# A retention layer and a leaky-ReLU layer on one core: the order of the products around the state sums, the first loads and the last bank

## The chip, the core and the metric

The kernel runs on one core of a Trainium2 chip. Its engines work side by side, each through its own queue in order: TensorE (PE; PEld is its loading of weights), VectorE (DVE), ScalarE (ACT), GpSimd (POOL) and SyncE (SP). SP and ACT also issue the DMAs in these runs. The metric is the device time of one execution in microseconds. Four runs of the kernel before gave 659.25, 658.70, 659.18 and 659.21, with a median of 659.19.

## The reference

Two layers in a row. The first is a recurrent retention over 768 steps, for 4 batch rows with 8 heads of 64 dimensions; the second is a pair of matrix products with a leaky ReLU between them, over the 3072 tokens of the first.

```python
for t in range(S):
    state = gamma[None, :, None, None] * state + np.einsum('bhd,bhe->bhde', k[:, :, t], v[:, :, t])
    y[:, :, t] = scale * np.einsum('bhd,bhde->bhe', q[:, :, t], state)
...
h = x @ w_in
g = np.maximum(0.01 * h, h)
return (g @ w_out).astype(np.float32)
```

## The kernel before

**Chunks and parts.** The sequence is cut into NC = 6 chunks c of 128 steps. For each chunk and each batch row b, the retention is four groups of small f32 products. `score` (L161) multiplies q and k within the chunk, and DVE masks the result (`masked`). `reads` (L215) multiplies q with the state of the chunk before; it uses 64x64 tiles of the array. `last_values` (L252) multiplies the scores with v for the second half of the chunk, with 128 rows and 64 columns of the array. `first_values` (L237) does it for the first half, with 64x64 tiles. `state` (L262) sums k times v for the new state, again with 128 rows and 64 columns; in the last chunk its loop is empty, because nobody needs that state. reads, both kinds of values and the state sums of one row share one tile in PSUM (`sums_at`): the tokens lie in a part of it, the state sums in another. A memset on POOL (`between`) stands between the reads of a row and its first_values, which waits for it. Afterwards DVE scales the tokens into x (`tokens_taken`) and updates the state (`state_taken`).

**The second layer.** 512 tokens of a chunk make a matrix x of 4 blocks. Both products of the second layer use a scheme of seven block products instead of eight, written in `seven` (L555) as M1 to M7; it needs sums and differences of blocks, which DVE makes. `hidden` is the first product with the leaky ReLU, `output` the second. The results of the seven go through four banks of PSUM, A to D. Names in the profile follow: A_h is bank A of hidden, C_o bank C of output. In the very first part of the work plain products are used instead (`direct`, shown as d at L599). In the last output of all, bank C is split in two: its two halves of 256 columns are two tiles, and after M3, the last product, each half is added and stored by itself (`takes_half`). M5 is the other product in that bank.

**Weights.** They arrive as 64-bit words. ACT makes the power of two of each number in three operations (`powers`, L485, at L495, L497 and L498), DVE the mantissa in three (L507, L512 and L519). A piece is 512 KB; the first four pieces are all that direct needs.

**Order.** The order is written by hand. Each engine's queue follows the order in which the code calls. The start is a straight list of calls (L744 to L857): loads, first scores, a product `spread` that spreads a table of decays over the partitions, its copy to `dec` (L821), which tokens_taken reads, then values, powers and mantissas of the first pieces. Chunk 1 is written out too, with `products_in_turn` (L863), which is called for rows 0 and 1 and then for rows 2 and 3. Chunks 2 to 5 use `visit` (L367), called for rows 0 and 1 of chunk 2 and rows 2 and 3 of chunk 5 in the midst of an output, and `visit_with_scores` for the others; the latter makes the state sums in a bank of its own, after last_values.

**Loads at the start.** SP issues q and k of row 0, v of row 0, weight pieces 0 and 1 and so on; ACT issues q and k of row 1, the table of decays and v of row 1 (L761). POOL multiplies v of rows 0 and 1 with their decays (L150) before PE uses it.

Of the kernel before, what the change touches and what calls it, by code (L numbers as in the profile page):

```python
# [9 lines left out]
FP32 = mybir.dt.float32  # L10
# [8 lines left out]
C = 128  # L19
# [4 lines left out]
def kernel(  # L24
# [38 lines left out]
    nc = tc.nc  # L63
    NC = S // C
# [3 lines left out]
    N = B * C // 2  # L68
# [5 lines left out]
    psum = ctx.enter_context(  # L74
        tc.tile_pool(name="psum", bufs=2, space=bass.MemoryType.PSUM))

    mask = const.tile([128, 3, C // 2], FP32, name="mask")
    dec = const.tile([128, HP * C + H + HP], FP32, name="dec")
# [28 lines left out]
    def block(k, i):  # L107

        if k < N_UNITS - 1:
            return unit(k)[:, i]  # L110
        return units[k][i // 2][:, i % 2] if i < 6 else last_s4[:, 0]
# [24 lines left out]
    def load_v(c, b, queue=nc.sync):  # L136
        queue.dma_start(out=heads[c, b][1][:, 1], in_=kv[c, b][:, 1])
# [20 lines left out]
    def two_banks(name):  # L158
        return psum.tile([128, 2, HP, C], FP32, tag="att", bufs=2, name=name)
# [55 lines left out]
    def reads(c, b):  # L215
        x = heads[c, b][0]
        ps = sums_at[c, b] = two_banks(f"yp_{c}_{b}")
        for j, m, i, a in pairs:
            mm = nc.tensor.matmul(ps[ts(i, 64), j, m, :], lhsT=st[b][ts(j, 64), a, :],  # L219
                                  rhs=x[ts(j, 64), 0, a, :], start=(m == 0), stop=False,  # L220
                                  skip_group_check=True)


        reads_done[c, b] = nc.gpsimd.memset(between, 0.0).ins
        tc.add_manual_dep(reads_done[c, b], mm.ins.name, IN_ORDER, reason="rows of the array")
# [3 lines left out]
    between = const.tile([128, 1], FP32, name="between")  # L229

    def values(c, b):
        if c == 0:
            sums_at[c, b] = two_banks(f"yp_{c}_{b}")
        last_values(c, b)
        first_values(c, b)
# [26 lines left out]
    def state(c, b):  # L262
        y = heads[c, b][1]
        sp = for_state(sums_at[c, b])
        for a in range(HP) if c < NC - 1 else ():
            sums_of(sp, y, a)
# [99 lines left out]

    def visit(c, b):  # L367

        for f in (reads, last_values, first_values, state):
            for i in range(2):  # L370
                f(c, b + i)
        for i in range(2):
            tokens_taken(c, b + i, xs[c][0])
        for i in range(2):
            state_taken(c, b + i, for_state(sums_at[c, b + i]))
        for i in range(2):
            if c + 1 < NC:
                ahead(c + 1, b + i)
# [69 lines left out]
            raws[n] = place.bitcast(I64)  # L448
        nc.sync.dma_start(out=raws[n], in_=weights[n])

    def next_powers(scratch=None):
        n = done["powers"]
        done["powers"] += 1
        if n < N_PIECES and f64:
            powers(n, scratch)

    def begin_mantissas(between=None):

# [23 lines left out]

    zs = {}

    def powers(n, scratch):  # L485

        top = raws[n].bitcast(U16).rearrange("p (h n four) -> p h n four", four=4, h=2)[:, :, :, 3]  # L490
        z = zs[n] = work.tile([128, 2, W // 2], I16, tag="z", bufs=3, name=f"z{n}")
        x = piece(n) if scratch is None else scratch


        nc.scalar.activation(x, top, AF.Prelu, alpha=float(BEND), scale=1.0 / 16,  # L495
                             bias=-7.5 / 16 - TOP)
        nc.scalar.activation(z, x, AF.Prelu, alpha=1.0 / BEND, bias=-float(BEND))  # L497
        nc.scalar.activation(z.bitcast(U16), z, AF.Relu, scale=128.0, bias=32768.0)  # L498

# [22 lines left out]
    def plus(out, a, b):  # L522
        nc.vector.tensor_tensor(out=out, in0=a, in1=b, op=ALU.add)  # L523
# [28 lines left out]
    ORDER = (0, 1, 2, 3, 4, 5, 6)  # L552
    FIRST = (0, 4, 1, 2, 3, 5, 6)

    def seven(tiles, name, takes, takes_half=None, order=ORDER):  # L555

        banks = {}  # L560
        which = [("M1", "A", 0, 0), ("M6", "B", 5, 5), ("M5", "C", 4, 4), ("M4", "D", 3, 6),
                 ("M2", "A", 2, 2), ("M7", "B", 1, 1), ("M3", "C", 6, 3)]
        for m, bank, sa, sb in (which[i] for i in order):
            first = bank not in banks
            split = takes_half is not None and bank == "C"
            if first and split:
                banks[bank] = [two_banks(f"{bank}{i}_{name}")[:, 0].rearrange("p a t -> p (a t)")[:, 0:N]
                               for i in range(2)]
            elif first:
                banks[bank] = psum.tile([128, 2, N], FP32, tag="ff", bufs=4, name=f"{bank}_{name}")  # L570
            ps = banks[bank]
            for i in range(2):
                half = ps[i] if split else ps[:, i, :]
                for n, (w, x, t) in enumerate(tiles):
                    rhs = x[:, sb] if sb < 4 else t[:, sb - 4]
                    for k in range(2):
                        nc.tensor.matmul(  # L577
                            half, lhsT=block(w, sa)[:, k, ts(i, 128)], rhs=rhs[:, k, :],
                            start=(first and (i == 0 or split) and n == 0 and k == 0),
                            stop=(n == len(tiles) - 1 and k == 1), skip_group_check=True)  # L580
                if split and m == "M3":
                    takes_half(i, half)
            if not (split and m == "M3"):
                takes(m, ps)
            yield
# [56 lines left out]
    def output(c, o, parts, first, final):  # L642

        got = {}
        at = f"{c}_{parts[0][0]}"

        def store(i):
            if final:
                nc.sync.dma_start(out=out[c, i], in_=o[:, i])

        def takes(m, ps):
            if m == "M1":
                got["m1"] = temp("m1", at)
                nc.scalar.copy(out=got["m1"], in_=ps)
            elif m == "M6":
                got["u2"] = temp("u2", at)
                plus(got["u2"], got["m1"], ps)
                if not first:
                    plus(o[:, 1], got["u2"], o[:, 1])
            elif m == "M5":  # L660
                got["m5"] = temp("m5", at)
                if first:
                    nc.scalar.copy(out=got["m5"], in_=ps)
                elif isinstance(ps, list):
                    for i in range(2):
                        plus(got["m5"][:, i], o[:, 3, i], ps[i])
                else:
                    plus(got["m5"], o[:, 3], ps)
            elif m == "M4":
                if first:  # L670
                    nc.scalar.copy(out=o[:, 2], in_=ps)
                else:
                    plus(o[:, 2], o[:, 2], ps)
            elif m == "M2":
                if first:
                    nc.scalar.copy(out=o[:, 0], in_=ps)
                else:
                    plus(o[:, 0], o[:, 0], ps)
                store(0)
            elif m == "M7":  # L680
                u3 = got["m1"]
                plus(u3, u3, ps)
                plus(o[:, 3], u3, got["m5"])
                store(3)
                plus(o[:, 2], u3, o[:, 2])
                store(2)
            elif m == "M3":
                plus(o[:, 1], got["u2"] if first else o[:, 1], ps)
                store(1)

        def takes_half(i, ps):
            plus(o[:, 1, i], o[:, 1, i], ps)
            nc.sync.dma_start(out=out[c, 1][:, i], in_=o[:, 1, i])

        return seven([(2 * u + 1, g, gd) for u, g, gd in parts], f"o{at}", takes,
                     takes_half if final and c == NC - 1 else None)


    def tile_x(c):
# [50 lines left out]
    x, t = xs[0]  # L750
    rows = t[:, 1:3].rearrange("p i k n -> p (i k n)")[:, 0 : decay.shape[1]]
    nothing = t[:, 0, 0, 0:64].bitcast(BF16)
    half = decay.shape[1] // 2
# [4 lines left out]
    nc.vector.memset(rows[:, half:], 0.0)  # L758
    nc.scalar.dma_start(out=rows[0:H], in_=decay)
    load_v(0, 0)  # L760
    load_v(0, 1, nc.scalar)  # L761
    load_piece(0)
    load_piece(1)
    load_qk(0, 2)
# [11 lines left out]
    for s in range(2):  # L776
        part = mask[ts(s, 64), 0 : 3 - s : 2 - s]
# [22 lines left out]
    spread = psum.tile([128, 2, N], FP32, tag="ff", bufs=4, name="spread")  # L800
# [3 lines left out]
    def scratch(name, n):  # L804
        return work.tile([128, 2, N], FP32, tag=name, name=f"{name}_x{n}")
# [12 lines left out]
    masked(0, 1)  # L818
    nc.tensor.matmul(spread.rearrange("p i n -> p (i n)"), lhsT=place, rhs=g_q, start=True,
                     stop=True, skip_group_check=True)  # L820
    nc.scalar.copy(out=dec[:, 0:n_gq], in_=spread.rearrange("p i n -> p (i n)"))  # L821
    values(0, 0)
    values(0, 1)
    next_powers(scratch("m1", 0))
    begin_mantissas(lambda: taken(0, 0, x))
    taken(0, 1, x)
    end_mantissas()
# [33 lines left out]
        masked(1, b)  # L861

    def products_in_turn(b):  # L863
        reads(1, b)
        values(1, b)
        reads(1, b + 1)
        values(1, b + 1)
        state(1, b)
        state(1, b + 1)

# [24 lines left out]
    next(later)  # L897
    last_sum(0)
    next_mantissas()
    products_in_turn(2)  # L900
    next_powers()
    run(steps, {})
    tokens_taken(1, 2, x1)
# [143 lines left out]
```

## Time and profile before

| What | Value |
|---|---|
| median of four runs | 659.19 us |
| the profiled execution's own time | 659.25 us |
| its span, first to last instruction | 657.4 us |
| granted TensorE clock | 1.000 |
| scores and tables, first products done | 5.70 to 9.5 us |
| PE's waits, all together | 2.2 us |
| last product ends | about 654.2 us |
| last store issued, span ends | 654.71, 657.4 us |

The span is what the profile shows of the execution; 1.85 us of the execution's own time lie outside it. PE's waits of 2.2 us fall into five places, all in the first 20 us. A row of the profile names the line of the code, the engine, the operation, and the tiles written and read; in a row of matmuls, "x16" counts passes, and a product in f32 takes two passes.

### The profile page before, as it was taken

To read this page: it belongs to the slowest core of one execution; us is meant where nothing else is said; L and a number is where in the kernel's file an instruction comes from. 1 tells how busy PE (TensorE), PEld (TensorE's weight loads), DVE (VectorE), ACT (ScalarE), POOL (GpSimd) and SP (SyncE) were. 2 spreads that over 40 slices of the span, in tenths; PEclk is the share of its full clock that TensorE was granted. 3 is DMA by queue.
4 is the path that set the end of the run, shared out by engine and by line. 5 is a ranking of instruction groups with operands and counts; after the bars stand their busy time and mean duration, and the time that the engine had idled before them with its cause. 6 is when DMAs were issued, how large, how long until landed. Compare 5 with 4: busy or idle time off the path is not lost.

```text
span 657.4 us, 11325 instructions
## 1 busy us (share of the span) xinstructions
PE 651.9 (99%) x4921; PEld 568.6 (86%) x4921; DVE 359.9 (55%) x587; ACT 176.3 (27%) x323; POOL 23.1 (4%) x45
## 2 busy tenths in 40 slices
PE   8999999999999999999999999999999999999998
PEld 5888888888888888888888889888888888888886
DVE  4779969889888674243436414526423344431342
ACT  4854555264261002202102211300220210211210
POOL 2000000000001020001001001001000100000000
PEclk9999999999999999999999999999999999999999
DMA  9921322322322650030022003005001001000001
GB/s 340 405 94 33 128 65 77 116 65 94 130 66 81 239 195 0 1 120 10 1 93 101 1 1 129 1 17 178 0 1 58 8 1 49 17 0 1 1 0 64
DMA packets 15761, 48.98 MB, mean 75 GB/s; under 512 B 1752, under 2 KB 2008, under 8 KB 15712
## 3 DMA queue, kind: packets, MB, share of 16 engines
q1 hardware_dynamic: 15408, 47.45, 20.5%
q8 instruction: 38, 0.62, 0.4%
q10 hardware_dynamic: 304, 0.81, 0.3%
q14 instruction: 11, 0.09, 0.0%
HBM read 41.97 MB, written 6.29 MB: 73 GB/s over the span
## 4 chain that ended last, share of the span: by engine, by line
PE 97%; ACT 1%; DMA 1%; DVE 0%; issue 0%
PE B_o L577 13%; PE A_o L577 13%; PE C_o L577 13%; PE A_h L577 12%; PE B_h L577 12%; PE C_h L577 12%; PE D_o L577 6%; PE D_h L577 6%; PE ap L182 3%; PE yp L255 2%; PE d L599 2%; PE yp L219 1%; PE yp L244 1%; PE sp L270 1%; DMA qk<-in_qk_dram 1%; PE yp L270 0%
## 5 line engine op out<-in xcount | busy, mean ns | idle before, releaser
L577 PE MATMUL A_h<-x,w 128*128 128x256 f32 x368 | 87.7, 381 | 0.0
L577 PEld LDWEIGHTS A_h<-x,w 128*128 128x128 f32 x368 | 69.3, 190 | 9.6
L577 PE MATMUL A_o<-g,w 128*128 128x256 f32 x288 | 68.1, 379 | 0.0
L523 DVE TENSOR_TENSOR m<-m,B_h 128x512 f32<-128x512 f32 x23 | 15.8, 687 | 94.4 <-PE B_h L577 94.4
L577 PEld LDWEIGHTS A_o<-g,w 128*128 128x128 f32 x288 | 54.6, 190 | 7.5
L612 ACT ACTIVATE g<-g 128x512 f32<-128x512 f32 x69 | 42.0, 630 | 66.0 <-DVE g L523 66.0
L617 ACT COPY m<-A_h 128x512 f32<-128x512 f32 x23 | 13.5, 586 | 170.2 <-PE A_h L577 150.0
L523 DVE TENSOR_TENSOR m<-m,B_o 128x512 f32<-128x512 f32 x16 | 11.0, 685 | 64.7 <-PE B_o L577 64.7
L577 PE MATMUL B_h<-t,w 128*128 128x256 f32 x184 | 43.6, 380 | 0.0
L577 PE MATMUL D_h<-t,w 128*128 128x256 f32 x184 | 43.5, 379 | 0.0
L577 PE MATMUL C_h<-x,w 128*128 128x256 f32 x184 | 43.5, 379 | 0.0
L577 PE MATMUL C_h<-t,w 128*128 128x256 f32 x184 | 43.5, 379 | 0.0
L577 PE MATMUL B_h<-x,w 128*128 128x256 f32 x184 | 43.5, 379 | 0.0
L577 PEld LDWEIGHTS B_h<-t,w 128*128 128x128 f32 x184 | 34.8, 190 | 5.1 <-DVE t L526 0.4
L577 PEld LDWEIGHTS D_h<-t,w 128*128 128x128 f32 x184 | 35.0, 190 | 4.8
L577 PEld LDWEIGHTS C_h<-x,w 128*128 128x128 f32 x184 | 35.0, 190 | 4.8
L577 PEld LDWEIGHTS C_h<-t,w 128*128 128x128 f32 x184 | 35.0, 190 | 4.8
L577 PEld LDWEIGHTS B_h<-x,w 128*128 128x128 f32 x184 | 35.0, 190 | 4.8
L526 DVE TENSOR_TENSOR gd<-g,gd 128x512 f32<-128x512 f32 x48 | 33.2, 692 | 1.7
L577 PE MATMUL B_o<-gd,w 128*128 128x256 f32 x144 | 34.0, 379 | 0.0
L577 PE MATMUL B_o<-g,w 128*128 128x256 f32 x144 | 34.0, 379 | 0.0
L577 PE MATMUL C_o<-gd,w 128*128 128x256 f32 x144 | 34.0, 379 | 0.0
(131 smaller groups left out, 983.7 us busy)
## 6 DMA issues: line engine op xcount, KB each, us to landing
raw<-in_weights_dram SPq DMA_DIRECT2D x31, 512.0 KB, 3.7
kv<-in_kv_dram SPq DMA_DIRECT2D x17, 512.0 KB, 5.1
out_dram<-o SPq DMA_DIRECT2D x23, 256.0 KB, 2.1
qk<-in_qk_dram SPq DMA_DIRECT2D x10, 512.0 KB, 4.5
o<-in_qk_dram SPq DMA_DIRECT2D x8, 512.0 KB, 4.7
in<-in_qk_dram SPq DMA_DIRECT2D x5, 512.0 KB, 8.4
in<-in_kv_dram SPq DMA_DIRECT2D x3, 512.0 KB, 8.0
in<-in_kv_dram SPq DMA_DIRECT2D x4, 256.0 KB, 8.5
```

The source lines that it names most:

```text
L182: nc.tensor.matmul(to, lhsT=x[ts(j, 64), 1, a, ts(late, 64)], rhs=x[ts(j, 64), 0, a, late * 64 :])
L219: mm = nc.tensor.matmul(ps[ts(i, 64), j, m, :], lhsT=st[b][ts(j, 64), a, :], rhs=x[ts(j, 64), 0, a, :], start=(m == 0), stop=False, skip_g ...
L244: mm = nc.tensor.matmul(ps[ts(i, 64), j, m, 0:64], lhsT=y[ts(s, 64), 1, 2 * a + j, :], rhs=am[ts(s, 64), j, m, 0], start=False, stop=True, ...
L255: nc.tensor.matmul(ps[ts(i, 64), j, m, 64:], lhsT=y[:, 1, 2 * a + j, :], rhs=am[:, j, m, 1 + (i ^ j)], start=(c == 0 and m == 0), stop=Tru ...
L270: nc.tensor.matmul(sp[ts(j, 64), a, :], lhsT=y[:, 0, 2 * a + j, :], rhs=y[:, 1, 2 * a + j, :], start=start, stop=True, skip_group_check=True)
L523: nc.vector.tensor_tensor(out=out, in0=a, in1=b, op=ALU.add)
L526: nc.vector.tensor_tensor(out=out, in0=a, in1=b, op=ALU.subtract)
L577: nc.tensor.matmul(half, lhsT=block(w, sa)[:, k, ts(i, 128)], rhs=rhs[:, k, :], start=(first and (i == 0 or split) and n == 0 and k == 0), ...
L599: nc.tensor.matmul(banks[r][:, i, :], lhsT=block(2 * u, r + 2 * kh)[:, k, ts(i, 128)], rhs=x[:, 2 * kh + th, k, :], start=(step == 0 and i ...
L612: nc.scalar.activation(g[:, i], g[:, i], AF.Prelu, alpha=0.01)
L617: nc.scalar.copy(out=got["m1"], in_=ps)
```

## The change

Four edits, and the names that go with them.

- `visit` calls state before first_values instead of after it.
- Rows 2 and 3 of chunk 1 go through a new function products_together, which does each of reads, last_values, state and first_values for both rows before the next. Rows 0 and 1 still use products_in_turn, which is only rewritten as loops.
- At the start, v of row 1 is loaded through SP's queue, between v of row 0 and weight piece 0, instead of ACT's. The copy of spread to dec is handed to the powers of piece 0 as `between`, and runs on ACT after the first of their three operations.
- In the last output, bank C's second half is cut in two again: PIECES lists 256 columns of the first half, and 128 and 128 of the second. The third piece is a new tile of the pool that the four banks come from. Products, adds and stores of M5 and M3 follow the pieces.

```diff
     def visit(c, b):
-        for f in (reads, last_values, first_values, state):
+        for f in (reads, last_values, state, first_values):
...
-    def powers(n, scratch):
+    def powers(n, scratch, between):
...
         nc.scalar.activation(x, top, AF.Prelu, alpha=float(BEND), scale=1.0 / 16,
                              bias=-7.5 / 16 - TOP)
+        if between is not None:
+            between()
         nc.scalar.activation(z, x, AF.Prelu, alpha=1.0 / BEND, bias=-float(BEND))
...
+    PIECES = ((0, 0, N), (1, 0, N // 2), (1, N // 2, N))
...
-                banks[bank] = [two_banks(f"{bank}{i}_{name}")[:, 0].rearrange("p a t -> p (a t)")[:, 0:N]
-                               for i in range(2)]
+                two = [two_banks(f"{bank}{i}_{name}")[:, 0].rearrange("p a t -> p (a t)")
+                       for i in range(2)]
+                two.append(psum.tile([128, 2 * N], FP32, tag="ff", bufs=4, name=f"{bank}_{name}"))
+                banks[bank] = [ps[:, 0 : z - a] for ps, (_, a, z) in zip(two, PIECES)]
...
-            for i in range(2):
-                half = ps[i] if split else ps[:, i, :]
+            places = zip(ps, PIECES) if split else ((ps[:, i, :], (i, 0, N)) for i in range(2))
+            for to, (i, a, z) in places:
...
-                            half, lhsT=block(w, sa)[:, k, ts(i, 128)], rhs=rhs[:, k, :],
+                            to, lhsT=block(w, sa)[:, k, ts(i, 128)], rhs=rhs[:, k, a:z],
...
-        def takes_half(i, ps):
-            plus(o[:, 1, i], o[:, 1, i], ps)
-            nc.sync.dma_start(out=out[c, 1][:, i], in_=o[:, 1, i])
+        def takes_piece(ps, i, a, z):
+            plus(o[:, 1, i, a:z], o[:, 1, i, a:z], ps)
+            nc.sync.dma_start(out=out[c, 1][:, i, a:z], in_=o[:, 1, i, a:z])
...
-    load_v(0, 1, nc.scalar)
+    load_v(0, 1)
...
-    nc.scalar.copy(out=dec[:, 0:n_gq], in_=spread.rearrange("p i n -> p (i n)"))
     values(0, 0)
     values(0, 1)
-    next_powers(scratch("m1", 0))
+    next_powers(scratch("m1", 0), lambda: nc.scalar.copy(
+        out=dec[:, 0:n_gq], in_=spread.rearrange("p i n -> p (i n)")))
...
+    def products_together(b):
+        for f in (reads, last_values, state, first_values):
+            for i in range(2):
+                f(1, b + i)
...
-    products_in_turn(2)
+    products_together(2)
```

## The prediction

> **What bounds the kernel now.** I read the page's busy shares first, then its chain of waits, then the list of what TensorE (PE) waited for, and only then the stages that the change touches.
>
> ```profile
> PE 651.9 (99%) x4921; PEld 568.6 (86%) x4921; DVE 359.9 (55%) x587; ACT 176.3 (27%) x323; POOL 23.1 (4%) x45
> PE 97%; ACT 1%; DMA 1%; DVE 0%; issue 0%
> PE d L599 <- DVE w L519: 0.7, 2, 0.4
> ```
>
> PE is busy 651.9 of 657.4 us and makes up 97% of the chain. The third line, from the list of waits, holds its only repeated wait after the first loads: 0.4 us at 13.28 and 0.3 at 19.13. So three things alone can shorten the span: less time inside PE's own sequence, the 0.3 us at 19.13, and the tail after PE's last product. Work moved on DVE, ACT, POOL or a queue counts only if PE comes to wait for it.
>
> The chain in order of time, in three windows (start us, us, what):
>
> ```profile
> 40.70 0.60 PE yp L219 x16
> 41.29 0.61 PE yp L255 x16
> 41.91 0.39 PE yp L244 x16
> 42.30 0.44 PE yp L219 x16
> 42.74 0.61 PE yp L255 x16
> 43.35 0.39 PE yp L244 x16
> 43.74 1.08 PE yp L270 x32
> ...
> 210.76 1.03 PE yp L219 x32
> 211.79 1.08 PE yp L255 x32
> 212.87 0.62 PE yp L244 x32
> 213.50 1.08 PE yp L270 x32
> ...
> 236.58 1.08 PE yp L255 x32
> 237.66 0.93 PE sp L270 x32
> ```
>
> The first window is the second call of products_in_turn, the second is visit(2, 0), the third a visit with scores. L219 is reads (64x64 tiles of the array), L255 last_values and L270 state sums (both 128x64), L244 first_values (64x64). The same 32 sums cost 1.08 after first_values and 0.93 after last_values. The 0.15 is the price of entering another shape of the array. Nothing waits in these windows.
>
> Start and tail, from the timeline (start, duration, engine, line):
>
> ```profile
> 9.56 0.59 ACT L821 COPY dec<-spread 128x512 f32<-128x512 f32 x1 [1.72 <-PE spread L819]
> 10.04 0.68 ACT L495 ACTIVATE m_x<-raw 128x512 f32<-128x512 uint16 x1
> 17.13 0.43 DVE L507 TENSOR_SCALAR w<-raw 128x512 uint32<-128x512 uint32 x1 [1.18 <-ACT z L497]
> 19.13 1.99 PE L599 MATMUL d<-x,w 128*128 128x256 f32 x8 [0.32 <-DVE w L519]
> ...
> 654.26 0.42 DVE L523 TENSOR_TENSOR o<-o,C_o 128x256 f32<-128x256 f32 x1 [1.11 <-PE C_o L577]
> 654.71 0.33 SPq L693 DMA_DIRECT2D out_dram<-o  x1
> ```
>
> ACT idles 1.72 us for the spread product and only then begins its weight work; DVE's L507 waits for that ACT chain, and PE at 19.13 for DVE. At the end stand one add of 0.42 us and one store of 128 KB.
>
> **What the Trainium skill says.** "TensorEngine Tiling (Array Packing)", Key Properties: a change of tiling mode drains TensorE. The trace agrees, at 0.15 us. "TensorE: Matmul & The Clock Gate", LDWEIGHTS: a load of weights takes its columns / 1.2 ns, so 107 ns for 128; Back-to-back issue gap: a product takes N/2.4 + 2.5 ns. The trace gives 216 ns per f32 pass of 256 columns (3.45 us for 16), which fits two cycles a column. A pass of 128 columns is then 109 ns (estimate), just longer than its load; no such pass is in this trace. "DMA: Bandwidth & Descriptors", Queues, rings and completion order: SP's and ACT's rings share the same 16 engines and alternate. The trace agrees: from 6.5 to 8.0 us ACT's queue has about a third of the traffic.
>
> **Part 1, products.** products_together(2) runs reads, last, state, first, for both rows each. From the rows above: 1.03 + 1.08 + 0.93 + 0.62 = 3.66. Before, the seven pieces sum to 4.12. Gain 0.46. The product that follows enters from first_values instead of state; such an entry is 3.65 for 16 passes at 546.97, against 3.45 without, so 0.20, and it was 0.19 (1.92 against 1.73): nothing. Cover: the tokens' adds on DVE need first_values of row 2, which ends about 43.97 instead of 42.30, but they waited for the sums until 44.41 before, so they start no later. t[:, 1] is ready at about 47.1, and B_h's weights load at 48.10, 0.46 earlier afterwards: slack 0.5 or more. Rows 2 and 3 were masked by 40.0.
>
> **visit.** 1.03 + 1.08 + 0.62 + 1.08 = 3.81 becomes 3.66: gain 0.15 in visit(2, 0). The call in the last chunk issues no sums, because state's loop is empty there: nothing. first_values also waits for POOL's memset after the reads (done at 212.0; it starts near 213.7): free.
>
> **Part 2, start.** load_v(0, 1) moves from ACT's queue to SP's, ahead of the first weight piece. It landed at 9.4 (POOL's decay of row 1 began at 9.46, waiting for it). Behind the first row's v, which landed at 6.73, its 256 KB need 0.65 us at 0.4 MB/us: about 7.4. Weight piece 0 landed at 8.60. All bytes up to and with it, 2.12 MB, are through at 7.8 by the page's rates, plus some 0.8 us as other loads show: 8.6 again. SP's later issues shift by one issue (0.42 us), under a queue that is full until 20 us. POOL then decays row 1 from 9.02, and PE's 0.3 us wait at 10.79 goes, only to become a longer wait at 13.28: there DVE's order from 10.66 decides (four operations to 13.22), which starts with row 0's tokens and is unchanged. So 0 for this edit.
>
> The copy of the spread table moves behind the first of ACT's three operations on piece 0. That one runs at 8.6 to 9.3, while ACT idled; the copy still starts at 9.56 with PE's spread product and is done before DVE needs it at 10.66. ACT's next operation starts at 10.06 instead of 10.75, and the whole chain up to L497 moves by 0.7 (its loads landed at 9.8, 11.85 and 13.1, each earlier than needed). L507 then starts at 16.4, L519 ends at 18.4. PE's natural start is 17.96 + 0.83 (scores, then d, as at 27.58 to 28.41) = 18.79, so DVE is no longer late. Gain 19.13 - 18.79 = 0.34. Behind it nothing holds PE: the sums need row 3 masked by 20.0 and k's landed by 20.4 against a start of 20.7.
>
> **Part 3, tail.** In the last output the bank C's second half is cut in two. Each of M5 and M3 turns 8 passes of 256 columns into 16 of 128. At the estimate of 109 ns that adds 0.02 each. The nearest row, last_values, has load and product of equal length too: 0.93/32 x 2 = 58 ns a pass, 2 over the formula. At that surcharge twice, 111.5 ns, 16 passes take 1.78 instead of 1.73. I take 0.06 each, 0.12 in all; ends 0.04 and 3.4 (a load not hidden at all, 107 x 32). D_o takes another bank, last written and read in the hidden product before: free. M5's third add stands in DVE's idle 1.3 us. The last add falls from 0.42 to 0.285 (512 columns cost 0.69 and 256 cost 0.42, so 0.27 per 256): gain 0.135. The last store halves to 64 KB: the 128 KB moved in about 0.5 us from 655.5, so up to 0.25 if time follows bytes, 0 if it follows packets, which stay 128. I take 0.15. SP's extra issue (0.33) fits between adds 0.9 us apart. Net gain 0.165.
>
> **Sum.** 0.46 + 0.15 + 0.34 + 0.165 = 1.12. The profiled run took 659.25 with a span of 657.4, so a span near 656.3. That run lies 0.06 above the median of the four, 659.19; from the median: **658.1 us**, 0.17% faster.
>
> **Rivals.** What a measurement here can tell from no change is about 0.2%, that is 1.3 us: faster is below 657.9, slower above 660.5.
> A, as summed, 658.1: chance 0.48.
> B, the ends give more: last store by bytes (0.25), no surcharge on the split (0.04), and another 0.2 to 0.3 at 13.28 if DVE and POOL hinder each other less. Sum 0.61 + 0.34 + 0.135 + 0.25 - 0.04 + 0.25 = 1.55: 657.6. For it: POOL's second decay took 1.27 against 1.04 with DVE busy beside it. Against: DVE's order begins with row 0. Chance 0.40, since the forecast lies only 0.2 from the bound.
> C, the start gives nothing: piece 0 lands after 9.4, so that the first ACT operation holds back the copy and DVE at 10.66; each 0.1 later costs 0.1. With 0.34 lost and as much as 0.2 on the store and the passes: 658.6. Against: the bytes say 8.6. Chance 0.07.
> D, slower: the weight loads of the 128-column passes stay exposed. It decides from 39 ns a pass (1.24 of other gain over 32 passes); fully exposed, 3.4 us, it gives 659.19 - 1.24 + 3.4 = 661.4. Against it: last_values hides equal loads. Chance 0.05.
>
> **Numbers.** Faster 0.40 (B), same 0.55 (A and C), slower 0.05 (D). The range reaches from 657.4 (B with its spread) to 658.9 (C and the runs' spread of 0.5); D is left out.
>
> **What would show it.** In the chain: L219, L255, L270, L244 near 40 us in 3.66, the same near 210. PE's wait at 19.1 gone, the one at 13.28 longer in total by what row 1 no longer waits. The copy of the spread still at 9.56, the first ACT weight operation before it. C_o passes of 128 columns 109 to 114 ns apart, the last add 0.29. I am wrong if the copy starts after 10, if a new PE wait stands between 44 and 50, or if the 128-column passes are over 130 ns apart.

## The result, and the profile after

The changed kernel takes 658.19 us (median of 41 runs, 657.78 to 658.81) against 658.98 for the kernel before (61 runs, 658.57 to 659.42), measured side by side: a ratio of 0.9989 with a 95% interval of 0.9984 to 0.9993. That is 0.79 us less, where the sum had said 1.12. The profiled execution took 658.68 us with a span of 656.9.

From the page of the changed kernel, PE's busy row and the shares of the chain; then from its list of what PE waited for (in all, times, longest):

```profile
PE 651.9 (99%) x4937; PEld 569.2 (87%) x4937; DVE 362.3 (55%) x589; ACT 176.3 (27%) x323; POOL 22.1 (3%) x45
PE 98%; DMA 1%; DVE 0%; ACT 0%; issue 0%
```

```profile
PE d L607 <- DVE w L523: 0.6, 1, 0.6
PE yp L244 <- issue: 0.4, 1, 0.4
```

The wait for DVE at 19.13 is gone; the one at the first plain product (13.3) is alone and longer, 0.6 instead of 0.4. The second row is new. It stands in first_values of chunk 0's row 3, and no semaphore is named for it. The chain of the changed kernel in four windows:

```profile
23.28 0.26 PE yp L244 x2
23.54 0.42 issue
23.96 0.46 PE yp L244 x11
...
41.10 1.03 PE yp L219 x32
42.13 1.08 PE yp L255 x32
43.22 0.93 PE yp L270 x32
44.15 0.62 PE yp L244 x32
...
210.93 1.03 PE yp L219 x32
211.97 1.08 PE yp L255 x32
213.05 0.93 PE yp L270 x32
213.98 0.62 PE yp L244 x32
...
344.57 0.93 PE sp L270 x32
```

Both reordered groups take 3.66, to the hundredth what the sum had. The pause is the first window: 0.42 of it stands in the chain as idle, and between the starts of two instructions of PE it is 0.64. The last window is for later: 32 sums without a break. From the timeline of the changed kernel, start and end of the program, and the first product of the output of chunk 0:

```profile
8.78 0.68 ACT L497 ACTIVATE m_x<-raw 128x512 f32<-128x512 uint16 x1 [0.81 <-DMA raw<-in_weights_dram]
9.69 0.59 ACT L831 COPY dec<-spread 128x512 f32<-128x512 f32 x1 [0.23 <-PE spread L827]
...
44.61 1.29 DVE L300 TENSOR_TENSOR x<-yp,dec 128x512 f32<-128x512 f32 x2 [1.74 <-PE yp L244]
...
58.01 0.68 DVE L527 TENSOR_TENSOR m<-m,B_h 128x512 f32<-128x512 f32 x1
58.74 0.73 PEld L585 LDWEIGHTS B_o<-gd,w 128*128 128x128 f32 x4 [0.36 <-DVE m L527]
...
653.15 1.68 SPq L701 DMA_DIRECT2D out_dram<-o  x3
654.18 0.29 DVE L527 TENSOR_TENSOR o<-o,C_o 128x128 f32<-128x128 f32 x1 [0.61 <-PE C_o L585]
```

The first weight operation of ACT runs while ACT had idled, and the copy is no later against the spread product than before. At 58.74 a weight load waits for DVE: B_o can't be written until `m<-m,B_h` has read the bank that it takes over. In the kernel before, the timeline has at that place:

```profile
44.41 1.29 DVE L300 TENSOR_TENSOR x<-yp,dec 128x512 f32<-128x512 f32 x2 [1.95 <-PE yp L270]
...
57.82 0.68 DVE L523 TENSOR_TENSOR m<-m,B_h 128x512 f32<-128x512 f32 x1
58.55 0.96 PEld L577 LDWEIGHTS B_o<-gd,w 128*128 128x128 f32 x5
```

There the bank came free at 58.50 and the load began at 58.55, the same 0.05 behind DVE as in the changed kernel. So it followed DVE there too, although no wait is shown: from the start of the last plain product (44.76 here, 44.70 in the changed kernel) to this load it is 13.79 here, 14.04 in the changed kernel, and 13.70 in e7_room below, where the bank is free early. The product behind the load was still on time here (13.92 from the same start, as in e7_room); the slack was almost used up.

Where the time went, by PE's starts in the two traces (us; the four stretches and the tail are differences of the marks):

| | before | after | change | of it |
|---|---|---|---|---|
| first plain product starts | 13.28 | 13.34 | +0.06 | first loads and scores; this start lies between 12.86 and 13.39 in the fourteen traces |
| to the third (the one DVE held at 19.13) | 5.86 | 5.47 | -0.39 | start |
| to the product after products_together | 25.63 | 25.90 | +0.27 | products -0.46, the stretch with the pause at 23.5 +0.73 (19.13 to 23.93 took 4.80, 18.81 to 24.34 takes 5.53) |
| to A_o after the visit | 169.75 | 169.83 | +0.08 | visit -0.15, wait for B_o +0.23 |
| to PE's end | 439.71 | 439.61 | -0.10 | split passes +0.12, and some -0.2 for a pause at 345 that this execution of before has and this one of after has not |
| PE's end to the span's end | 3.15 | 2.79 | -0.36 | last add -0.13, landing of the store -0.16, what SP does behind it -0.07 |
| span | 657.37 | 656.94 | -0.43 | |

This execution gained less than the median. Two of these rows are losses that the prediction did not have: the wait at 58.7, and the pause at 23.5, which, as the runs below show, is not in every execution.

### The profile page after: what moved, and what is told of

Read it like the earlier page. It is cut to its first block, busy times and chain, and to the rows that moved or that the text cites. A ratio compares the mean times of both kernels' runs of the same rounds, so it can differ in the third digit from the quotient of the medians.

```text
span 656.9 us, 11361 instructions
## 1 busy us (share of the span) xinstructions
PE 651.9 (99%) x4937; PEld 569.2 (87%) x4937; DVE 362.3 (55%) x589; ACT 176.3 (27%) x323; POOL 22.1 (3%) x45
## 4 chain that ended last, share of the span: by engine, by line
PE 98%; DMA 1%; DVE 0%; ACT 0%; issue 0%
PE B_o L585 13%; PE A_o L585 13%; PE C_o L585 13%; PE A_h L585 12%; PE B_h L585 12%; PE C_h L585 12%; PE D_o L585 6%; PE D_h L585 6%; PE ap L182 3%; PE d L607 2%; PE yp L255 2%; PE yp L219 1%; PE yp L244 1%; PE sp L270 1%; DMA qk<-in_qk_dram 1%; PE yp L270 0%
## 5 line engine op out<-in xcount | busy, mean ns | idle before, releaser
L585 PE MATMUL C_o<-g,w 128*128 128x256 f32 (+1 forms) x148 | 34.2, 373 | 0.0
L585 PE MATMUL C_o<-gd,w 128*128 128x256 f32 (+1 forms) x148 | 34.2, 373 | 0.0
```

The lines of the kernel that those rows point to most:

```text
L585: nc.tensor.matmul(to, lhsT=block(w, sa)[:, k, ts(i, 128)], rhs=rhs[:, k, a:z], start=(first and (i == 0 or split) and n == 0 and k == 0), ...
```

## The experiments

Each was timed against the kernel before on the same chip, in five rounds. The intervals of the ratios are some 0.8 to 1.1 us wide, so that gains of 0.2 to 0.4 us are read from the traces and not from the medians. "Plain products" below means the time from the first plain product (13.3) to the one behind the products of rows 2 and 3 (44.7): 31.49 in before, 31.37 in after; with 0.46 and 0.39 (the start's gain up to the third plain product) both kept it would be 30.64.

### The parts alone

e1_products has only the new order in visit and products_together, e2_start only the load and the copy, e3_end only PIECES.

```diff
-        for f in (reads, last_values, first_values, state):
+        for f in (reads, last_values, state, first_values):
...
-    products_in_turn(2)
+    products_together(2)
```

> The kernel before with the new order of the products alone (products_together for rows 2 and 3 of chunk 1, state before first_values in visit). Both theories expect the same here: 0.61 us less PE work, 0.46 at 40 us and 0.15 at 211 us, so a time 0.6 us below before (ratio 0.9991), provided that no wait opens behind it. A smaller gain would mean that a wait did open.

```diff
-    load_v(0, 1, nc.scalar)
+    load_v(0, 1)
...
-    nc.scalar.copy(out=dec[:, 0:n_gq], in_=spread.rearrange("p i n -> p (i n)"))
...
-    next_powers(scratch("m1", 0))
+    next_powers(scratch("m1", 0), lambda: nc.scalar.copy(
+        out=dec[:, 0:n_gq], in_=spread.rearrange("p i n -> p (i n)")))
```

> The kernel before with the start alone (v of row 1 through SP's queue, the copy of spread after the first weight operation). Theory F (the gain of 0.34 us at 19.1 is lost again where PE stands still in the middle of row 3's first_values near 23.5, because its next block of instructions has not arrived): PE's wait at 19.1 is gone, a pause of 0.3 us or more stands near 23.3 to 24, and the time is within 0.2 us of before or slower. Rival G (the pause in the profile of the changed kernel was chance): no pause, time 0.3 us below before.

```diff
+    PIECES = ((0, 0, N), (1, 0, N // 2), (1, N // 2, N))
...
-        def takes_half(i, ps):
-            plus(o[:, 1, i], o[:, 1, i], ps)
-            nc.sync.dma_start(out=out[c, 1][:, i], in_=o[:, 1, i])
+        def takes_piece(ps, i, a, z):
+            plus(o[:, 1, i, a:z], o[:, 1, i, a:z], ps)
+            nc.sync.dma_start(out=out[c, 1][:, i, a:z], in_=o[:, 1, i, a:z])
```

> The kernel before with the last bank in three pieces alone. As predicted: 0.165 us below before. By the trace of the changed kernel (passes of the bank 0.06 longer in each of M5 and M3, tail from PE's end to the span's end 0.43 shorter): 0.3 us below. Under theory F the products give 0.6 and the end 0.2 to 0.3, which is the whole measured gain of 0.8; under rival G the end must give nothing or cost 0.1, since products and start would be 0.95 by themselves.

| | median | before | ratio, interval |
|---|---|---|---|
| e1_products | 658.71 | 659.08 | 0.9993, 0.9985 to 1.0002 |
| e2_start | 658.79 | 659.08 | 0.9995, 0.9987 to 1.0003 |
| e3_end | 658.75 | 659.08 | 0.9995, 0.9987 to 1.0003 |

None of the three is told from no change by its interval alone; the traces say more. In e1_products plain products take 31.08, 0.41 less; then B_o waits as in the changed kernel, and from the last plain product to A_o after the visit it takes 169.84 instead of 169.75, although the visit is 0.15 shorter. In e2_start the third plain product comes after 5.46, 0.40 less than before, and yet plain products take 31.36: all but 0.13 is given back before 44, 0.12 of it in row 3's values and 0.16 between 28 and 35, where the reads of row 1 stand. The pause of 0.3 or more that F forecast is not there, and the median is 0.29 below before: taken alone, this run is what G forecast. In e3_end the tail is 2.78, 0.37 less. The medians' gains add up to 0.99, the whole had 0.79, a difference within these intervals.

### Is the pause a late block of instructions?

The pause stands at the same place in PE's own count: its record (loads, products and waits on semaphores counted from 0) stops before number 705. The Trainium skill, "Runtime: NRT & Kernel Launch", Instruction fetch mechanics, says that an engine reads its program in blocks of 16 KiB, 256 instructions, through a DMA queue of its own while it executes the block before, and that this is mostly hidden. The page of this kernel has such a queue:

```profile
q8 instruction: 39, 0.64, 0.4%
```

39 packets with 0.64 MB are 16 KB each, and 4937 loads and 4937 products need some 39 blocks of 256. That PE stands still because its next block has not arrived is theory F; G was at first that the pause is chance, and from e5_move on that it belongs to row 3's work. Four runs bear on it. e4_relief is the changed kernel with the loads of rows 0 and 1 of chunk 1 and of weight pieces 4 and 5 held back:

```diff
-        if n != 3:
+        if n > 1 and n != 3:
             load_piece(n + 4 if n < 3 else n + 3)
...
-    load(1, 0, unit_tile(LATE[2], "in10"))
-    load(1, 1, unit_tile(LATE[1], "in11"))
...
-    masked(0, 2)
+    seen = masked(0, 2)
+    later_load = load(1, 0, unit_tile(LATE[2], "in10"))
+    tc.add_manual_dep(later_load.ins, seen.ins.name, IN_ORDER, reason="not before this")
+    load(1, 1, unit_tile(LATE[1], "in11"))
+    load_piece(4)
+    load_piece(5)
```

> The changed kernel with the loads of rows 0 and 1 of chunk 1 and of weight pieces 4 and 5 held back on SP until row 2 of chunk 0 is masked (about 16 us instead of 13.3), so that 0.5 MB less stands in the DMA engines when PE asks for its next instructions. Theory F, with the fetch queued behind the data: the fetch that started at 21.5 in the changed kernel starts near 20, the pause near 23.5 is gone, and the time is 0.3 to 0.7 us below the changed kernel (1.1 to 1.5 below before). Rival G, or F with a fetch that does not queue behind data: no difference from the changed kernel, 0.8 below before.

658.32 against 659.08 (0.9987, 0.9980 to 0.9993). The packet with the block (the last on that queue before number 705) began at 21.10 instead of 21.46, and the pause stayed, 0.64 between two starts. If the block queued behind these loads, F forecast a start near 20 and no pause; neither came, and one trace doesn't settle more.

```diff
-    for b in range(B):
+    for b in range(2):
         first_state(b, sums0)
...
     run(steps, {})
+    for b in range(2, B):
+        first_state(b, sums0)
     taken(0, 3, x)
```

> The changed kernel, with the state sums of rows 2 and 3 of chunk 0 moved behind the last step of the first plain product, so that 64 instructions of PE less stand ahead of row 3's values. Theory F (PE stops in row 3's first_values at its 705th instruction because its next block of instructions is not there yet): the 705th then falls into work that PE reaches about 0.8 us later, so the pause of 0.4 to 0.6 us at 23.3 is gone or far smaller, and the time is 0.3 to 0.7 us below the changed kernel. Theory G (the pause belongs to row 3's values, to an engine or a bank that the trace does not show as a wait): the pause stays in row 3's first_values, and the time is that of the changed kernel or above it.

```diff
-    keep_busy(10)
+    for _ in range(20):
+        nc.tensor.matmul(idle.rearrange("p i (two n) -> p (i two) n", two=2)[:, 0:2], lhsT=nothing,
+                         rhs=nothing.unsqueeze(1).to_broadcast([128, 2, 128]),
+                         start=True, stop=True, skip_group_check=True)
```

> The changed kernel, with the ten warm-up products of 512 columns at the start made as twenty of 256 columns: 20 more PE instructions, no more time. Theory F: the pause stays at PE's 705th instruction, which is now 20 instructions earlier in the program, so it falls on row 3's last_values instead of first_values, some 0.5 us earlier, and is longer by about as much; the time is 0.1 to 0.6 us above the changed kernel. Theory G: the pause stays at the same product of row 3's first_values, and the time is the same.

e5_move took 658.30 against 659.13 (0.9988, 0.9981 to 0.9994), e6_pad 658.12 (0.9984, 0.9978 to 0.9991). In neither is there a pause in row 3's values. So e6_pad's forecast of a longer one, and of more time, failed, and so did the 0.3 to 0.7 us below the changed kernel that e5_move was to give: it is 0.83 below before, and the changed kernel 0.79. In e6_pad the block arrived early, at 20.85. In e5_move, where number 705 now lies in the sums behind row 3's values, it came 3.25 us after its packet (21.30). Worked out from the traces, for all kernels whose 705th instruction lies in row 3's values (us; instructions in order of their starts, "gap" is the time since the one before; in e2_start and e9_after a lag of 0.12 is spread over the passes there):

```
             packet ends  #705 starts  after packet   gap
before          21.79        23.55        1.76        0.00
e1_products     21.29        23.18        1.89        0.00
e3_end          22.09        23.75        1.66        0.00
e6_pad          20.85        22.55        1.70        0.00
e10_mask        21.35        22.77        1.43        0.00
e2_start        21.65        23.10        1.46        0.02
e9_after        21.44        22.94        1.50        0.02
e12_turn        22.07        23.43        1.37        0.54
after           22.54        23.96        1.42        0.64
e11_best        22.36        23.88        1.51        0.64
e4_relief       22.18        23.70        1.52        0.64
e7_room         22.57        24.10        1.53        0.73
```

Number 705 never starts sooner than 1.37 us after its packet, and where there is a gap it starts 1.37 to 1.53 after. Before, e1_products and e3_end, with the old start, come later than that anyway; with the start 0.39 earlier PE arrives at the edge, and the packet's own lateness, 20.85 to 22.57, decides. The packet's time is nothing that PE's work there could set: after and e9_after are the same program, and their packets end at 22.54 and 21.44.

The same sign stands 5120 instructions on. 5825 is 705 plus 20 blocks, and falls into the sums of a visit with scores. From the chains of e6_pad and of e9_after at that place:

```profile
343.81 0.28 PE sp L270 x9
344.10 0.04 issue
344.13 0.92 PE sp L270 x23
```

```profile
343.67 0.58 PE sp L270 x19
344.25 0.31 issue
344.56 0.62 PE sp L270 x13
```

In e9_after the break is behind 19 passes; in e6_pad, whose program has 20 more instructions ahead, it is behind 9 (0.26 between two starts, of which the chain counts 0.04): ten loads and ten products earlier in the program, the same number in the count. The changed kernel's own profile has no break there (0.93 for all 32), before has 0.20 of one. That number is reached 1.24 to 1.55 us after its packet in all fourteen traces. So the place of the pause goes with the count and its end with the packet, and not with row 3's work: F holds in what it says of blocks, and G falls. No run moves the packet by itself; the cause rests on these two agreements.

e8_both shows a cure and its price. It has e5_move's edit and that of e7_room below, which tests theory H, that the wait at B_o takes back 0.24 of the gain of the products:

> The changed kernel with both moves: the state sums of rows 2 and 3 of chunk 0 behind the first plain product, and state_taken of rows 2 and 3 of chunk 1 behind the hidden product. If F and H hold, the two gains add: 0.5 to 0.9 us below the changed kernel, that is 1.2 to 1.6 below the kernel before. If only H holds, 0.2 to 0.3 below the changed kernel.

658.12 against 659.13 (0.9985, 0.9979 to 0.9992). Its packet came late, at 22.29, but number 705 was 2.47 us behind it, and no pause followed. Yet plain products took 31.08, as in e5_move. In e5_move's chain the sums of chunk 0 take 1.08 twice instead of 2.02, and the plain products around them 1.92 twice instead of 3.65: 0.33 more, the price of one more entry into each. The rest is at the reads of row 1, below. The expected 0.5 to 0.9 us below the changed kernel is not reached; by the medians it is where e7_room is alone.

### The wait for the bank at 58.7

```diff
-    state_taken(1, 2, for_state(sums_at[1, 2]))
-    state_taken(1, 3, for_state(sums_at[1, 3]))
     run(later, {0: [next_mantissas], 1: [lambda: differences(*parts[0][1:])],
                 2: [next_powers], 3: [lambda: add_sums(1)]})
+    state_taken(1, 2, for_state(sums_at[1, 2]))
+    state_taken(1, 3, for_state(sums_at[1, 3]))
```

> The changed kernel, with state_taken of rows 2 and 3 of chunk 1 called after the whole hidden product instead of before it, so that 1.6 us of VectorE work less stands ahead of add_sums(1). Theory H (products_together gains 0.46 us, of which 0.24 is lost at 58.5, where the first product of B_o waits for VectorE, which is busy without a break from the tokens on): no wait at the first B_o, from the end of the plain products to A_o at 214 us 169.6 instead of 169.84, and the time 0.2 to 0.3 us below the changed kernel. Rival: the wait at B_o is for something else, or another wait takes its place: the same time as the changed kernel.

658.08 against 659.13 (0.9984, 0.9978 to 0.9991). From its timeline:

```profile
56.59 0.68 DVE L527 TENSOR_TENSOR m<-m,B_h 128x512 f32<-128x512 f32 x1
...
58.57 1.05 PEld L585 LDWEIGHTS B_o<-gd,w 128*128 128x128 f32 x5
```

The bank is free at 57.27, the wait has gone, and from the last plain product to A_o after the visit it takes 13.92 + 155.69 = 169.61, with 169.83 in after and 169.75 in before. So the visit's 0.14 is there, and the wait had cost 0.22. H holds by the trace; that the median is 0.26 further below before than the changed kernel's agrees, but lies within the intervals.

### What is late where the pause is not

e9_after is the changed kernel again.

> The changed kernel once more, for a second profile and as the yardstick of the two runs beside it. Theory F' (the pause at PE's 705th instruction is real, but whether it costs 0, 0.1 or 0.7 us differs from execution to execution with the time at which the block of instructions arrives; where it costs nothing, the reads of row 1 at 32.2 wait for masked(1, 1) instead, because ScalarE's chain behind the load of chunk 1's v, which starts near 23.1 whatever PE does, is no earlier): either the pause at 23.3 is there, and no wait at 32.2, or the other way round; from the first plain product to the last one at about 44 it takes 30.9 to 31.4 us, against 30.64 if the start and the products gave all that was summed. Rival: neither is there, and those 30.64 are reached. Time 658.1 to 658.4.

658.48 against 659.08 (0.9990, 0.9983 to 0.9996). At number 705 it lags by 0.12 only (0.51 in its chain for passes that take 0.39), and plain products take 30.87, 0.23 more than 30.64. Its gain is 0.60 where the first comparison gave 0.79. The rest of the loss is at the reads of row 1, in its chain:

```profile
32.07 0.03 issue
32.10 0.67 PE yp L219 x16
```

The sixteen passes of row 0's reads took 0.45, and row 1's took 0.58 in before and 0.57 in after, although PE comes to them later there than here (32.59 and 32.99, here 32.10): the wait is in every trace with this order, and the forecast that it comes only where the pause is missing failed. From the timelines of before, DVE's mask of row 1 and PE's reads of row 1:

```profile
31.59 0.95 DVE L204 TENSOR_TENSOR am<-ap,mask 128x768 f32<-128x768 f32 x1
...
32.59 0.67 PE L219 MATMUL yp<-in,states 64*64 64x128 f32 x16
```

The reads begin 0.05 behind the mask's end. In e6_pad, whose plain products take 30.89, the chain names what row 1's reads waited for:

```profile
23.18 2.03 ACT in L154 x8
25.21 0.96 ACT g L612 x2
26.17 0.83 ACT in L154 x4
27.00 0.02 issue
27.03 1.07 ACT in L154 x4
28.10 0.59 ACT w L497
...
31.23 0.96 DVE am L204
32.20 0.04 issue
32.24 0.67 PE yp L219 x16
```

The reads don't use the mask. But scores and reads take their PSUM tiles in turn from one pool of two (`two_banks`), and by the order of the calls the reads of row 1 get the tile of row 1's scores, which the mask has to read first. ACT starts its decay of chunk 1's v when that load has landed, at 22.93 to 23.43 in the traces, whatever PE does; then come the products' leaky ReLU, the next row's decay, a weight piece's powers, DVE's mantissas and, last, the mask of row 1. A start that brings PE there earlier waits for the end of that row: against 0.44 without a wait, the reads lose 0.14 in before and 0.26 in e9_after. Two edits shorten it. The first lets the mask go ahead of the mantissas:

```diff
     score(1, 1)
     next_powers()
+    masked(1, 1)
     next_mantissas()
-    masked(1, 1)
     next_powers()
```

> The changed kernel with masked(1, 1) called before next_mantissas instead of after it, so that VectorE masks row 1's scores of chunk 1 at about 30.5 instead of 31.3 to 32.2. If the start's gain is lost at the reads at 32.2 behind that mask, it now stays where the pause at 23.5 is absent: 30.6 to 30.7 us from the first plain product to the last, and 0.1 to 0.25 us below the changed kernel in the median. If the pause is there in every execution, the mask is hidden behind it and nothing changes; if the weights' mantissas, 0.95 us later, are needed at once, a new wait follows within 15 us and the time is the same or above.

658.58 against 659.08 (0.9990, 0.9982 to 0.9999), nothing below e9_after beside it. The reads are on time, and a new wait stands further on, in the chain:

```profile
31.90 0.44 PE yp L219 x16
...
37.24 0.39 issue
37.63 0.89 PE ap L182 x22
```

DVE's mantissas, moved behind the mask, made state_taken of row 1 late (read at 37.12 to 37.53), and row 3's score follows at 37.63. By the same order of the pool of two it takes the tile that state_taken of row 1 reads; the trace doesn't name it. Together with e7_room's edit:

> Both that edit and state_taken of rows 2 and 3 of chunk 1 behind the hidden product (the run e7_room). No wait at 32.2 and none at B_o at 58: 0.3 to 0.5 us below the changed kernel, 1.1 to 1.4 below the kernel before. If only the B_o wait mattered: 0.2 below the changed kernel.

658.68 against 659.08 (0.9993, 0.9986 to 0.9999): a miss. Its profile has the wait at 38.7 (0.65 between two instructions), the pause at number 705 (0.64) and 0.24 at 5825, and no wait at B_o. The second edit moves ACT's work in place of DVE's, on top of e7_room:

```diff
-    decay_v(1, 1, nc.scalar)
     next(steps)
     score(1, 1)
     next_powers()
+    decay_v(1, 1, nc.scalar)
     next_mantissas()
```

> The run e7_room (state_taken of rows 2 and 3 of chunk 1 behind the hidden product), and ScalarE's eight decays of row 1's v of chunk 1 called after the three power operations of the next weight piece instead of before them. The powers then start near 26 instead of 28, VectorE's three mantissa operations end about 30.8 instead of 31.3, and masked(1, 1) stands about 0.4 us earlier, with no VectorE work put behind it as in e10_mask. Expected if the reads at 32.2 wait for that mask: sixteen passes of the second reads in 0.44 us instead of 0.67, no new wait at 37.6, and 0.2 us below e7_room, about 1.2 below the kernel before. If the weight piece has not landed by 26, or if v of row 1 is then late for its values at 32.9: nothing gained.

657.69 against 659.07 (17 runs; 0.9978, 0.9971 to 0.9986), 1.38 us less than before, and the fastest of all. It was not run beside the changed kernel, whose own gains over before were 0.79 and 0.60; its upper bound 0.9986 just overlaps the changed kernel's lower one, 0.9984, and its interval overlaps most of e7_room's, so the medians alone don't show what the second edit adds. From its chain, and then ACT's first power operation from its timeline:

```profile
22.86 0.25 PE yp L244 x2
23.11 0.32 issue
23.43 0.46 PE yp L244 x11
...
32.57 0.44 PE yp L219 x16
```

```profile
26.88 0.68 ACT L497 ACTIVATE w<-raw 128x512 f32<-128x512 uint16 x1 [0.44 <-DMA raw<-in_weights_dram]
```

The reads of row 1 take 0.44, there is no wait at 37.6 and none at B_o, though this execution has the pause (0.54). But the powers began at 26.88 and not near 26, as the weight piece had not landed, and the mask ended at 32.16. The reads start at 32.39; without the pause of 0.54 PE would be there about 0.5 earlier (estimate), and the wait would be back. No trace shows that case.

## Why the prediction was nearly right

The forecast of 658.1 was 0.1 off, but its gain was 0.33 too large: the kernel before ran at 658.98 here, 0.21 below the four runs that the forecast started from. That the two errors cancel in part is luck. The parts were nearly right; two steps, both on what waits behind a gain, were not.

- **Products.** 3.66 and 3.66, as summed. The step that failed is the cover: "slack 0.5 or more" was worked out for B_h's load at 48.10, and the chain on DVE was not followed beyond it. DVE has next to no idle time (two gaps of 0.1) from its tokens at 44.4 until `m<-m,B_h` at 58, and there hardly any slack was left. PE came 0.46 earlier, but DVE's tokens only 0.20: against the last plain product they started 0.35 before it in before, 0.09 before it in after. Of that 0.26 PE waited 0.22, as e7_room shows. So the term 0.46 was worth 0.24. The forecast named 44 to 50 as the stretch to watch; the wait was 8 us later.
- **Visit.** 0.15 forecast, 0.14 in e7_room.
- **Start.** Each step before 19 came as told: copy behind the first weight operation, no wait at 19.13, 0.39 instead of 0.34. "Behind it nothing holds PE" failed. Only the inputs of the sums and of row 3 were looked at. At row 3's values the block of instructions is at the edge, and at 32.2 the mask had no slack: the reads of row 1 waited for it already in before, which no list of waits shows and the prediction did not see. In e9_after and e6_pad 0.14 to 0.16 of the 0.39 is left; in after's profile the start cost 0.34 net. The load of v was not run by itself; the spread product's end to the first plain product is 3.76 in before and 3.69 in after, so nothing here speaks against its value of 0.
- **Ends.** The split cost 0.12, as forecast, 0.06 in each of M5 and M3: the passes of 128 columns start 111 to 112 ns apart. The estimate of 109 is worked out from "TensorE: Matmul & The Clock Gate", Back-to-back issue gap, which gives that formula for an isolated product; the surcharge that the prediction laid on it, to 111.5, was needed. (The row of 0.93 from which it took the surcharge is that of the state sums, not of last_values.) The add gave 0.13. The tail gave 0.36. The store landed 1.54 us after its issue instead of 1.70, so it gave 0.16, where 0.15 was taken. The other 0.07 was not forecast: behind the landing SP runs two semaphore instructions, 0.06 apart, instead of three before it drains.
- **Rivals.** B fell: the store gave 0.16 and not 0.25, the split did not come free, and from the spread product to 13.28 only 0.07 was gained. C had the start give nothing, for another cause (a late first piece), which the trace refutes: the piece was used at 8.78. But in after's profile the start did give nothing. D fell: the short passes hid their loads. One load lasts 190 to 192 ns in the traces, where the prediction reckoned 107, but the loads start every 110 to 112 ns, like the passes.

With the measured terms, products 0.24, visit 0.15, ends 0.24 and start 0.15 where the pause is short make 0.78; with a pause as in the profile it is 0.3. That 0.78 meets the median of 0.79 is no proof: of the eight traces with the new start in which number 705 lies in row 3's first_values, five have a gap of 0.54 or more, and how often it comes in the executions without a trace is not known. The second comparison, 0.60, lies between the two sums.

## What to carry to other kernels

- When the bound engine is made earlier by a few tenths, follow every engine that feeds it, without idle time, to the first place where it hands over a result or a bank; the slack is what is left there, not at the first consumer.
- A row that takes longer than its twin (0.67 against 0.45 for the same sixteen passes) can be a wait that the list of waits doesn't show.
- A dense stretch of short instructions can outrun the fetch of the program. Count instructions there, as well as time, before a start is made earlier.

## What was not expected of the hardware

The refill of instructions, mostly hidden by the section named above, was not hidden here: PE stood still before a block of 256 instructions for up to 0.7 us, in two places, and where it did the block began 1.27 to 1.54 us after its 16 KB packet ended. At number 5569 of the changed kernel, PE entered a block at 341.75; the packet of the next ran from 342.09 to 343.37, and that block began at 344.92, 3.17 us after the entry. In the products of 256 columns a block lasts 27.6 us (59.93 to 87.56), and nothing of it shows. What makes the packet at the start come at 19.8 to 21.5 in different executions was not found: holding back loads did not settle it.
